# Grouped-query attention on one core: the first transposes, copies and products of the first chunk in quarters

## The chip, the cores and the metric

The kernel runs on one core of a Trainium2 chip. The metric is the device time of one execution in microseconds (us), the slowest core's (here the only one's). PE is the matrix engine, PEld its loads of weights, DVE the vector engine, ACT the scalar engine, SP the engine that issues nearly all DMAs (loads from and stores to memory). A load "lands" when the last of its data is in.

## The reference

Two independent problems, A and B, of the same shape, whose outputs are joined:

```python
B, Sq, D = 16, 32, 1024          # 512 tokens
Hq, Hkv, Sk, Dh = 32, 4, 512, 128
q = (x @ wq)                     # 512 x 1024 by 1024 x 4096
scores = einsum("bhqd,bhkd->bhqk", q, k) * Dh ** -0.5    # k, v: one head for 8 query heads
o = einsum("bhqk,bhkd->bhqd", softmax(scores), v)
out = o @ wo                     # 512 x 4096 by 4096 x 1024
```

All tensors are bfloat16. The change touches only the first microseconds of the first step, `x @ wq` of problem A.

## The kernel before

The kernel keeps PE busy with one long stream of matmuls. At the start there is nothing to multiply: the kernel loads x, transposes it on PE (its products contract over the partitions, so it puts D there), copies it from PSUM, the buffers that it has PE write to, to SBUF, where the loads land and PE's operands lie, and loads the weights. Until then PE multiplies constants ("warm-ups"; those that fill a wait between other matmuls are called "fillers").

x is loaded in chunks of two D-blocks, the first chunk in two token halves; weights follow in the order of use. All these loads are issued by SP, one after the other:

```python
load_x(0, 0, TT // 2)            # D-blocks 0 and 1, tokens 0..255
load_w0(0, 1, 0, NF // 2)        # "first weights":  D-block 0, heads 0..2
load_x(0, TT // 2, TT)           # D-blocks 0 and 1, tokens 256..511
load_w0(0, 1, NF // 2, NF)       # "second weights": D-block 0, heads 3..5
load_w0(1, 2, 0, NF)             # "third weights":  D-block 1, heads 0..5
load_x(2, 0, TT)
# ... (more weights, the rest of x by transposing DMAs; cut)
load_wq(0, 2, 0, 2)
load_k(0)                        # four transposing DMAs
load_wq(0, 2, 2, 4)
# ... (cut)
```

P is 128, TT is 4 (tokens in blocks of 128), NF is 6 (heads in the first group), HALF is 4. The start itself:

```python
def transpose_x(d0, t0, t1):
    for d, copy in ((d0, nc.vector.tensor_copy), (d0 + 1, nc.scalar.copy)):
        ps = psum.tile([P, NTOK], BF16, name="xT_ps", tag="ob")
        for tt in range(t0, t1):
            nc.tensor.transpose(ps[:, tt * P:(tt + 1) * P], x_sb[:, tt, d * P:(d + 1) * P], ident[:])
        ts = slice(t0 * P, t1 * P)
        copy(out=xT[0][:, d, ts], in_=ps[:, ts])

# first_heads(heads, dcs, t0, t1): q[h] += w[dc, h].T @ xT[dc, tokens t0..t1], one matmul per head and dc

warm_up(22)
transpose_x(0, 0, TT // 2)
warm_up(3)
first_heads((0, 1), (0,), 0, TT // 2)
transpose_x(0, TT // 2, TT)
first_heads((2,), (0,), 0, TT // 2)
warm_up(1)
first_heads((0, 1, 2), (0,), TT // 2, TT)
first_heads((3, 4, 5), (0,), 0, TT // 2)
first_heads((3, 4, 5), (0,), TT // 2, TT)
first_heads(range(0, NF - 2), (1,))       # the first that needs the third weights
# ... (cut)
```

## Time and profile before

| | before |
|---|---|
| time, median of 3 runs | 343.97 us (343.52 to 344.53) |
| span of the profiled run | 342.1 us |
| PE busy | 338.1 us, 99% of the span |
| first matmul; last matmul starts | 0.93 us; 338.74 us |
| array rate doubles, by the distances of matmuls | about 6.44 us |

The page of the kernel before: the first lines (busy time, share of the span, instructions of each engine) and the chain of work that ended last.

```profile
span 342.1 us, 5510 instructions
## 1 busy us (share of the span) xinstructions
PE 338.1 (99%) x2128; PEld 214.6 (63%) x2128; DVE 265.6 (78%) x336; ACT 185.7 (54%) x209; POOL 46.6 (14%) x206
...
## 4 chain that ended last, share of the span: by engine, by line
PE 99%; ACT 0%; issue 0%; ACTq 0%
```

PE makes up 99% of that chain. A busy PE need not be a fast PE, though: in this trace PE counts as 99% busy although the first 5.5 us of it, from 0.93 to about 6.44 us, run at half rate. The starts of matmuls tell more. The timeline of PE from 3.25 to 6.95 us (start, us from first start to last end, what, how many):

```profile
3.03 0.42 PE L515 MATMUL q_ps<-const-bfloat16-1.0 128*128 128x128 bf16 x2
3.29 0.61 PE L523 MATMUL xT_ps<-ident,x_sb 128*128 128x128 bf16 x4
3.69 0.53 PE L515 MATMUL q_ps<-const-bfloat16-1.0 128*128 128x128 bf16 x3
4.07 0.59 PE L533 MATMUL q_ps<-xT,w_sb 128*128 128x256 bf16 x2
4.44 0.63 PE L523 MATMUL xT_ps<-ident,x_sb 128*128 128x128 bf16 x4
4.87 0.42 PE L533 MATMUL q_ps<-xT,w_sb 128*128 128x256 bf16 x1
5.08 0.31 PE L515 MATMUL q_ps<-const-bfloat16-1.0 128*128 128x128 bf16 x1
5.25 1.93 PE L533 MATMUL q_ps<-xT,w_sb 128*128 128x256 bf16 x10
```

L515 is a warm-up, L523 a transpose, L533 a product. The DVE timeline shows the two copies that the products of the first and second token half wait for:

```profile
3.72 0.29 DVE L527 COPY xT<-xT_ps 128x256 bf16<-128x256 bf16 x1 [2.76 <-PE xT_ps L523]
4.90 0.29 DVE L527 COPY xT<-xT_ps 128x256 bf16<-128x256 bf16 x1 [0.89 <-PE xT_ps L523]
```

The first copy ends at 4.01 us and the product starts at 4.07; the second ends at 5.19 and the product starts at 5.25.

### The profile page before, as it was taken

To read this page: it belongs to the slowest core of one execution; us is meant where nothing else is said; L and a number is where in the kernel's file an instruction comes from. 1 tells how busy PE (TensorE), PEld (TensorE's weight loads), DVE (VectorE), ACT (ScalarE), POOL (GpSimd) and SP (SyncE) were. 2 spreads that over 40 slices of the span, in tenths; PEclk is the share of its full clock that TensorE was granted. 3 is DMA by queue.
4 is the path that set the end of the run, shared out by engine and by line. 5 is a ranking of instruction groups with operands and counts; after the bars stand their busy time and mean duration, and the time that the engine had idled before them with its cause. 6 is when DMAs were issued, how large, how long until landed. Compare 5 with 4: busy or idle time off the path is not lost.

```text
span 342.1 us, 5510 instructions
## 1 busy us (share of the span) xinstructions
PE 338.1 (99%) x2128; PEld 214.6 (63%) x2128; DVE 265.6 (78%) x336; ACT 185.7 (54%) x209; POOL 46.6 (14%) x206
## 2 busy tenths in 40 slices
PE   8999999999999999999999999999999999999996
PEld 7456666666666666666666666666666666666555
DVE  1047988888888889888888888798888888889540
ACT  2067666676666666676655554555454555555110
POOL 0001111101111111111101212222122100111100
DMA  6999999899999998999999856999439996430001
GB/s 194 253 243 183 284 261 256 173 232 269 299 234 248 238 252 231 251 304 303 281 319 259 191 125 180 283 323 211 129 104 306 350 194 139 103 96 17 17 17 33
DMA packets 128093, 71.70 MB, mean 210 GB/s; under 512 B 75840, under 2 KB 127296, under 8 KB 128064
## 3 DMA queue, kind: packets, MB, share of 16 engines
q1 hardware_dynamic: 127536, 70.21, 84.7%
q0 software_dynamic: 384, 1.05, 0.9%
q8 instruction: 17, 0.28, 0.3%
q14 instruction: 12, 0.10, 0.1%
q10 hardware_dynamic: 144, 0.07, 0.1%
HBM read 50.86 MB, written 2.10 MB: 155 GB/s over the span
## 4 chain that ended last, share of the span: by engine, by line
PE 99%; ACT 0%; issue 0%; ACTq 0%
PE f_ps L320 32%; PE q_ps L301 28%; PE ob L425 16%; PE s_ps L357 16%; PE q_ps L533 4%; PE q_ps L515 1%; PE xT_ps L523 0%; ACT o_sb L329 0%; ACTq L329 0%
## 5 line engine op out<-in xcount | busy, mean ns | idle before, releaser
L365 ACT ACTIVATE p_sb<-s_ps,shift 128x1024 bf16<-128x1024 f32 x128 | 142.6, 1114 | 97.8 <-PE s_ps L357 82.0
L376 DVE TRANSPOSE_TENSOR_REDUCE parts<-p_sb 128x32 f32<-128x1024 bf16 x128 | 158.8, 1240 | 19.2 <-ACT p_sb L365 17.6
L320 PE MATMUL f_ps<-wo_sb,oT 128*128 128x512 bf16 (+1 forms) x544 | 131.8, 366 | 0.0
L301 PE MATMUL q_ps<-xT,wq_sb 128*128 128x512 bf16 x448 | 117.4, 379 | 0.0
L425 PE MATMUL ob<-p_sb,v_sb 128*128 128x256 bf16 x512 | 76.8, 273 | 0.0
L357 PE MATMUL s_ps<-qT,kT 128*128 128x256 bf16 x512 | 76.8, 273 | 0.0
L320 PEld LDWEIGHTS <-oT 128*128 128x128 bf16 x544 | 53.2, 98 | 35.8
L357 PEld LDWEIGHTS <-kT 128*128 128x128 bf16 x512 | 56.9, 113 | 28.3
L301 PEld LDWEIGHTS <-wq_sb 128*128 128x128 bf16 x448 | 43.8, 98 | 31.7 <-DMA wq_sb<-in_A_wq_dram 0.2
L425 PEld LDWEIGHTS <-v_sb 128*128 128x128 bf16 x512 | 50.1, 98 | 20.0
L447 DVE TENSOR_TENSOR oT<-r,ob 128x512 bf16<-128x512 f32 x64 | 43.9, 686 | 21.9 <-PE ob L425 20.8
L411 DVE STREAM_TRANSPOSE r<-rall 128x512 f32<-128x512 f32 x64 | 44.2, 691 | 1.1
L309 ACT CAST qT<-q_ps 128x512 bf16<-128x512 f32 x56 | 32.6, 583 | 15.4 <-PE q_ps L301 15.4
L394 POOL COPY half<-cs 64x32 f32<-64x32 f32 x32 | 6.5, 204 | 227.4 <-DVE cs L384 227.3
L329 ACT CAST o_sb<-f_ps 128x512 bf16<-128x512 f32 (+1 forms) x17 | 9.5, 558 | 24.6 <-PE f_ps L320 24.6
L533 PE MATMUL q_ps<-xT,w_sb 128*128 128x512 bf16 (+1 forms) x70 | 15.4, 377 | 0.0
L384 DVE TENSOR_REDUCE cs<-parts 128x32 f32<-128x128 f32 x32 | 12.0, 376 | 1.1
L406 DVE RECIPROCAL rall<-sums 128x32 f32<-128x32 f32 x32 | 10.2, 320 | 3.3 <-POOL sums L403 3.3
L533 PEld LDWEIGHTS <-w_sb 128*128 128x128 bf16 x70 | 7.2, 104 | 6.9
L561 DVE CAST qT<-q_ps 128x512 bf16<-128x512 f32 x4 | 2.5, 683 | 10.2 <-PE q_ps L533 10.2
L331 POOL DMA_DIRECT2D out_dram<-o_sb x8 | 4.6, 574 | 34.7 <-ACT o_sb L329 34.6
L395 POOL TENSOR_TENSOR half<-half,cs 64x32 f32<-64x32 f32 x32 | 7.8, 242 | 2.6
(25 smaller groups left out, 46.3 us busy)
## 6 DMA issues: line engine op xcount, KB each, us to landing
v_sb<-in_A_v_cache_dram SPq DMA_DIRECT2D x16, 512.0 KB, 6.5
wq_sb<-in_B_wq_dram SPq DMA_DIRECT2D x8, 1024.0 KB, 6.0
wo_sb<-in_A_wo_dram SPq DMA_DIRECT2D x8, 1024.0 KB, 6.4
v_sb<-in_B_v_cache_dram SPq DMA_DIRECT2D x16, 512.0 KB, 4.4
wo_sb<-in_B_wo_dram SPq DMA_DIRECT2D x8, 1024.0 KB, 8.4
wq_sb<-in_A_wq_dram SPq DMA_DIRECT2D x5, 1024.0 KB, 6.3
wq_sb<-in_A_wq_dram SPq DMA_DIRECT2D x2, 512.0 KB, 5.8
kT<-in_A_k_cache_dram SPq DMA_TRANSPOSE x64, 4.5
```

Source lines behind the costliest of these rows:

```text
L301: nc.tensor.matmul(ps[:], lhsT=w[:, dc, (h % 4) * DH:(h % 4 + 1) * DH], rhs=xT[pr][:, dc, :], start=(dc == 0), stop=(dc == DC - 1),)
L309: nc.scalar.copy(out=qT[pr, g][:, :, hl, :], in_=ps[:].rearrange("p (b s) -> p b s", s=SQ),)
L320: nc.tensor.matmul(ps[:, 0:width], lhsT=oT[pr, tt][:, h, :], rhs=wo_tiles[pr, nh, h // REP][:, h % REP, off:off + width], start=(h == 0), ...
L357: nc.tensor.matmul(s_ps[:, c, :], lhsT=kT[:, i % GRP, c, :], rhs=qT[pr, g][:, b, :, :].rearrange("p h s -> p (h s)"), start=True, stop=True,)
L365: nc.scalar.activation(out=p_sb[:], in_=s_ps[:], func=ACTF.Exp, bias=shift[:], scale=SCALE)
L376: nc.vector.tensor_reduce(out=parts[k][:, q, :, :].rearrange("p c h -> p (c h)"), in_=st[i]["p"][:].rearrange("p c (h s) -> p (c h) s", s=SQ),
L384: nc.vector.tensor_reduce(out=cs[:], in_=parts.pop(k)[:].rearrange("p q c h -> p q h c"), axis=AX.X, op=ALU.add,)
L406: nc.vector.reciprocal(out=rall[:, k, :], in_=quad.pop(k)[:])
L411: nc.vector.transpose(out=r[:].rearrange("p n s -> p (n s)"), in_=rall[:, k, o * 2 * REP:(o + 1) * 2 * REP] .unsqueeze(2).to_broadcast([P, ...
L425: nc.tensor.matmul(ob[j][:, q, :], lhsT=v_sb[:, i % GRP, c, :], rhs=st[i]["p"][:, c, :], start=(c == 0), stop=(c == KC - 1),)
L447: nc.vector.tensor_tensor(out=out, in0=rcp.pop(j)[:].rearrange("p (q h) s -> p q h s", h=REP), in1=ob.pop(j)[:].rearrange("p q (h s) -> p ...
L533: nc.tensor.matmul(first_q[h][:, ts], lhsT=w0[dc // HC][:, dc % HC, h * DH:(h + 1) * DH], rhs=xT[0][:, dc, ts], start=(dc == 0 and t0 == 0 ...
```

## The change

The intent: get the first product going earlier, with fewer fillers. D-block 0 of the first token half is transposed and copied in two quarters of 128 tokens, so that the first copy is shorter and begins after one transpose rather than two; the products of heads 0 to 2 run by quarters too; and the second half's transposes stand between the two quarters. One filler goes. D-block 1 of the first half gets a PSUM buffer of its own (`spare`).

```diff
+            spare = psum.tile([P, NTOK], BF16, name="xT_ps", tag="proj")
             first_q += [psum.tile([P, NW], FP32, name="q_ps", tag="proj")[:] for _ in range(2)]
...
-            def transpose_x(d0, t0, t1):
-                for d, copy in ((d0, nc.vector.tensor_copy), (d0 + 1, nc.scalar.copy)):
+            def transpose_x(d, t0, t1, copy, ps=None):
+                if ps is None:
                     ps = psum.tile([P, NTOK], BF16, name="xT_ps", tag="ob")
... (the body unindented, warm-ups written to first_q[HALF]; cut)
             warm_up(22)
-            transpose_x(0, 0, TT // 2)
-            warm_up(3)
-            first_heads((0, 1), (0,), 0, TT // 2)
-            transpose_x(0, TT // 2, TT)
-            first_heads((2,), (0,), 0, TT // 2)
+            for tt in range(2):
+                transpose_x(0, tt, tt + 1, nc.vector.tensor_copy)
+            transpose_x(1, 0, 2, nc.scalar.copy, spare)
+            warm_up(2)
+            first_heads((0, 1, 2), (0,), 0, 1)
+            transpose_x(0, 2, TT, nc.vector.tensor_copy)
+            transpose_x(1, 2, TT, nc.scalar.copy)
+            first_heads((0, 1, 2), (0,), 1, 2)
             warm_up(1)
-            first_heads((0, 1, 2), (0,), TT // 2, TT)
-            first_heads((3, 4, 5), (0,), 0, TT // 2)
-            first_heads((3, 4, 5), (0,), TT // 2, TT)
+            first_heads((0, 1, 2), (0,), 2, TT)
+            first_heads((3, 4, 5), (0,), 0, 2)
+            first_heads((3, 4, 5), (0,), 2, TT)
```

More of the change, by code (lines that the diff above doesn't have):

```diff
@@ L515, in warm_up @@
                     nc.tensor.matmul(
-                        first_q[NF - 1][:, 0:P], lhsT=warm, rhs=warm, start=True, stop=True
+                        first_q[HALF][:, 0:P], lhsT=warm, rhs=warm, start=True, stop=True
                     )
-            def transpose_x(d0, t0, t1):
-                for d, copy in ((d0, nc.vector.tensor_copy), (d0 + 1, nc.scalar.copy)):
+            def transpose_x(d, t0, t1, copy, ps=None):
+                if ps is None:
                     ps = psum.tile([P, NTOK], BF16, name="xT_ps", tag="ob")
-                    for tt in range(t0, t1):
-                        nc.tensor.transpose(
-                            ps[:, tt * P:(tt + 1) * P], x_sb[:, tt, d * P:(d + 1) * P], ident[:]
-                        )
-                    ts = slice(t0 * P, t1 * P)
-                    copy(out=xT[0][:, d, ts], in_=ps[:, ts])
+                for tt in range(t0, t1):
+                    nc.tensor.transpose(
+                        ps[:, tt * P:(tt + 1) * P], x_sb[:, tt, d * P:(d + 1) * P], ident[:]
+                    )
+                ts = slice(t0 * P, t1 * P)
+                copy(out=xT[0][:, d, ts], in_=ps[:, ts])
             def first_heads(heads, dcs, t0=0, t1=TT):
@@ L541, in fast_path @@
             warm_up(22)
-            transpose_x(0, 0, TT // 2)
-            warm_up(3)
-            first_heads((0, 1), (0,), 0, TT // 2)
-            transpose_x(0, TT // 2, TT)
-            first_heads((2,), (0,), 0, TT // 2)
+            for tt in range(2):
[6 more added lines that the diff above has]
+            first_heads((0, 1, 2), (0,), 1, 2)
             warm_up(1)
-            first_heads((0, 1, 2), (0,), TT // 2, TT)
-            first_heads((3, 4, 5), (0,), 0, TT // 2)
-            first_heads((3, 4, 5), (0,), TT // 2, TT)
+            first_heads((0, 1, 2), (0,), 2, TT)
+            first_heads((3, 4, 5), (0,), 0, 2)
+            first_heads((3, 4, 5), (0,), 2, TT)
             first_heads(range(0, NF - 2), (1,))
-            transpose_x(2, 0, TT)
+            transpose_x(2, 0, TT, nc.vector.tensor_copy)
+            transpose_x(3, 0, TT, nc.scalar.copy)
             first_heads(range(NF - 2, NF), (1,))
```

## The prediction

> **What bounds the kernel now.** TensorE. The page gives PE 338.1 us busy of a 342.1 us span (99%), and the chain that ended last is 99% PE. Because matmul ends are modelled, I also took the starts of all 2128 matmuls from the trace and subtracted, from each start-to-start distance, the distance a matmul of that width shows when the array is fast (columns/2.4 ns plus 2.4 ns, which the trace shows throughout: 512 columns 215.7 ns, 128 columns 56 ns). After 10 us the excess is below 0.01 us per 10 us up to the last matmul: no wait on a DMA, a copy or a buffer remains there. All excess, 2.69 us, lies before 10 us. So time saved or lost at the start arrives undiminished at the end.
>
> **What the first 10 us show (timeline).** The 22 warm-ups start at 0.93 us, 107 ns apart. First x half landed 3.24; four transposes 3.29 to 3.69; three warm-ups; DVE copy (128x256, 0.29 us) ends 4.01; first multiplication 4.07; second x half landed 4.16; its transposes start 4.44; second DVE copy ends 5.19, next multiplication 5.25. 256-column matmuls are 213 ns apart until about 6.35 us and 110 ns after it: the array runs at half rate until then. The two waits for copies look like 56 ns each, but the matmul after each comes only 165 ns later instead of 213, so they cost about 10 ns each. The warm-ups already fill them.
>
> **What the change does.** PE work: one warm-up less (25 where 26 were; 107 ns slow, 56 ns fast); three 256-column matmuls become six of 128 (three more, about 2.4 ns each when fast). Transposes are unchanged. DVE's first copy becomes two of 128x128; from the measured 0.29 us (256 columns) and 0.42 us (512) I estimate 0.22 us each, on an idle engine. ACT's copies keep their size. The spare PSUM buffer swaps the two single-bank q buffers; their later users come in the same order.
>
> New timeline, estimated: transposes 3.29 to 3.69, two warm-ups to 3.90, first copy ends about 3.84 so the first quarter starts at 3.90 with no wait; three quarters to 4.22, by when the second x half is in by some 0.03 us (landing 4.16 plus 0.04 us to the load of weights); transposes to 4.65; second quarters to 4.97; warm-up to 5.08; DVE copy ends 4.97; multiplication of the second half at about 5.08 instead of 5.25. The catch-up of 165 ns disappears, so the true gain is about 0.12 us at the slow rate.
>
> If the rate doubles at the same moment as before, that progress is worth only half later: about 0.06 us, 0.02% of the time. All of it is on the critical path. The next loads used (second weights landed 4.99, used 5.84; third 6.21, used 6.80; x 7.06, used 7.66) have 0.5 us or more to spare, so they do not take it back.
>
> **What is larger than the change.** The moment of doubling. [...] An estimate from it: 1 us later costs 0.5 us, which is as wide as the three runs (343.52 to 344.53).
>
> **Predicted:** 343.9 us, 343.2 to 344.6. Faster by over 2%: 0.005; within 2%: 0.99; slower: 0.005.
>
> **Signs.** First quarter near 3.9; second-half transposes near 4.2; multiplication of the second half near 5.1; PE excess after 10 us still none; 2130 matmuls.
>
> **What would make it wrong.** The second x half landing late, stalling the transposes now placed earlier; a DVE copy slower than 0.3 us; [...].

## More of the kernel before

The starts inside a group (from the trace) are 107 ns apart for 128 columns and 213 ns for 256 until about 6.44 us, and 56 and 110 ns after it: this is the "doubling" of the rate.

## The result

| | before | after |
|---|---|---|
| time, median of 6 runs | 343.94 us (343.42 to 344.53) | 343.88 us (343.28 to 345.40) |
| ratio, 95% interval | | 1.0004 (0.9984 to 1.0024) |
| span of the profiled run | 342.1 us | 343.6 us |
| rate doubles, by the distances of matmuls | about 6.44 us | about 4.36 us |
| waits of PE after 10 us, from the starts of matmuls | none | 1.49 us at 25.3, 0.28 us at 42.5 |

A ratio is the mean time of one kernel's runs over that of the other's of the same rounds, so it is not quite the ratio of the medians.

The time is the same. The two profiles, however, differ much more than the times: the profiled run of the changed kernel was its slowest, 345.40 us, and its chain no longer is PE alone.

```profile
span 343.6 us, 5515 instructions
## 1 busy us (share of the span) xinstructions
PE 337.7 (98%) x2130; PEld 213.7 (62%) x2130; DVE 265.9 (77%) x337; ACT 185.9 (54%) x209; POOL 47.1 (14%) x206
...
## 4 chain that ended last, share of the span: by engine, by line
PE 87%; SPq 9%; DMA 2%; issue 0%; ACT 0%; ACTq 0%
```

SP's queue holds 9% of the chain, that is, loads were late. The timeline of PE of the same stretch as before (L516 is now a warm-up, L524 a transpose, L534 a product):

```profile
3.03 0.42 PE L516 MATMUL q_ps<-const-bfloat16-1.0 128*128 128x128 bf16 x2
3.29 0.61 PE L524 MATMUL xT_ps<-ident,x_sb 128*128 128x128 bf16 x4
3.69 0.42 PE L516 MATMUL q_ps<-const-bfloat16-1.0 128*128 128x128 bf16 x2
3.91 0.53 PE L534 MATMUL q_ps<-xT,w_sb 128*128 128x128 bf16 x3
4.28 0.42 PE L524 MATMUL xT_ps<-ident,x_sb 128*128 128x128 bf16 x4
4.53 0.33 PE L534 MATMUL q_ps<-xT,w_sb 128*128 128x128 bf16 x3
4.70 0.22 PE L516 MATMUL q_ps<-const-bfloat16-1.0 128*128 128x128 bf16 x1
4.97 1.14 PE L534 MATMUL q_ps<-xT,w_sb 128*128 128x256 bf16 x9
6.49 0.82 PE L534 MATMUL q_ps<-xT,w_sb 128*128 128x512 bf16 x3 [0.39 <-DMA w_sb<-in_A_wq_dram]
```

The first product starts at 3.91 us instead of 4.07, as intended. The array doubled its rate 0.45 us later, 2.1 us earlier than in the profile before: the four transposes at 4.28 us, during which this happened, take 0.42 us where they took 0.63. That earliness is then spent: the product of the second half at 4.97 us comes only when the DVE copy below is done (4.91 us), and the products with the third weights wait until 6.49 us, because those weights landed at 6.45 us.

```profile
3.62 0.36 DVE L528 COPY xT<-xT_ps 128x128 bf16<-128x128 bf16 x2 [2.66 <-PE xT_ps L524]
4.62 0.29 DVE L528 COPY xT<-xT_ps 128x256 bf16<-128x256 bf16 x1 [0.65 <-PE xT_ps L524]
```

The waits of 20 to 31 us (who waited for what: us in total, times, longest us):

```profile
PEld L301 <- DMA wq_sb<-in_A_wq_dram: 1.7, 1, 1.7
PE q_ps L301 <- DMA wq_sb<-in_A_wq_dram: 1.3, 1, 1.3
```

And the traffic of the DMA queues from 13 to 21 us in 40 slices of 0.2 us, first before, then after:

```profile
GB/s 317 164 307 264 343 407 297 274 282 300 276 283 271 288 123 44 37 38 35 17 18 112 288 262 256 291 93 106 193 193 107 49 15 125 33 33 74 128 218 289
```

```profile
GB/s 339 442 236 338 254 325 320 312 294 289 294 305 269 300 258 101 3 0 0 0 10 8 10 13 20 20 18 20 20 17 18 191 291 227 287 288 85 164 215 122
```

In both, the traffic nearly stops when the first transposing loads of keys run, at 15.8 to 16 us. The longest single packet there took 1.47 us before and 3.31 us after. With the longer stop, the loads that landed from 19.4 to 30 us did so 1.7 to 2.2 us later than in the profile before, among them the weights that PE waits for at 25.3 us (landed 25.27).

So the profiles alone give two readings. Theory A: the moment of doubling and the length of the stop are chance, and the change itself saves at most some hundredths of a microsecond. Theory B: the change brings the early doubling and the longer stop, a gain and a loss that cancel. And within theory A, a second question: does the little that the change saves reach the end, as I predicted (theory 1), or is it swallowed by a load (theory 2)?

### The profile page after: what moved, and what is told of

Read it like the earlier page. It is cut to its first block, busy times and chain, and to the rows that moved or that the text cites. A ratio compares the mean times of both kernels' runs of the same rounds, so it can differ in the third digit from the quotient of the medians.

```text
span 343.6 us, 5515 instructions
## 1 busy us (share of the span) xinstructions
PE 337.7 (98%) x2130; PEld 213.7 (62%) x2130; DVE 265.9 (77%) x337; ACT 185.9 (54%) x209; POOL 47.1 (14%) x206
## 4 chain that ended last, share of the span: by engine, by line
PE 87%; SPq 9%; DMA 2%; issue 0%; ACT 0%; ACTq 0%
PE f_ps L320 32%; PE q_ps L301 24%; PE ob L425 16%; PE s_ps L357 15%; SPq L275 6%; DMA v_sb<-in_A_v_cache_dram 2%; SPq L477 1%; SPq L471 1%; SPq L246 1%; SPq L465 0%; SPq L283 0%; ACT o_sb L329 0%; SPq L711 0%; ACTq L329 0%
## 5 line engine op out<-in xcount | busy, mean ns | idle before, releaser
L534 PE MATMUL q_ps<-xT,w_sb 128*128 128x512 bf16 (+2 forms) x73 | 14.9, 357 | 0.4 <-DMA w_sb<-in_A_wq_dram 0.4
L534 PEld LDWEIGHTS <-w_sb 128*128 128x128 bf16 x73 | 7.0, 100 | 7.3 <-DMA w_sb<-in_A_wq_dram 0.7
```

The source lines that it names most:

```text
L534: nc.tensor.matmul(first_q[h][:, ts], lhsT=w0[dc // HC][:, dc % HC, h * DH:(h + 1) * DH], rhs=xT[0][:, dc, ts], start=(dc == 0 and t0 == 0 ...
```

## The experiments

Twelve kernels ran, in three groups of four, each group on one chip. In the lists "use" is the start of the first matmul with the third weights, "landing" the landing of those weights, both from the trace. "Doubling" is the step of the granted clock as the trace records it (it recorded none in the first two profiles).

### Both kernels again: e1, g4 (before), e2, g3 (after)

No edit.

e1, kernel before: 

> The kernel before, unchanged, run again for its scatter. Theory A (what separates the two profiles is chance: the moment at which the array's rate doubles, and the length of a stop in the DMA traffic near 16 us): the time is 343.3 to 344.5 us, ratio 1.000, and the new profile shows the doubling somewhere between 4.2 and 7.7 us and a stop of 1 to 3.5 us near 16 us, either of them clearly different from the first profile's 6.35 us and 1.5 us. Theory B (the change itself causes the earlier doubling and the longer stop): doubling again within 0.3 us of 6.35 us and a stop again of about 1.5 us, no wait of PE at 25 us.

g4, kernel before: 

> The kernel before for a third profile: a doubling before 5 us here would show that the kernel before, too, then waits for the third weights at 6.1 to 6.5 us, and for its copies; one after 6 us shows again no wait for loads at all. Ratio 0.999 to 1.001: the scatter that an unchanged kernel has.

e2, changed kernel: 

> The changed kernel, unchanged, run again. Theory A: doubling and stop differ from the first profile's 4.25 us and 3.3 us, and the waits of PE (0.55 us at 6.5, 1.49 us at 25.3, 0.28 us at 42.5) shrink or vanish with them; ratio to before 0.999 to 1.001. Theory B: doubling at 4.0 to 4.5 us and the wait of 1 us or more at 25 us come back.

g3, changed kernel: 

> The changed kernel for a third profile. If the stop of 3.3 us near 16 us and the wait of 1.49 us at 25 us in its first profile were chance, as nine other profiles with stops of 1.2 to 1.8 us suggest, the stop is again 1.2 to 2 us and no wait over 0.1 us is left after 10 us. If the changed kernel brings them, they are back. Doubling anywhere from 4.2 to 7.7 us; the time fits 0.93 us + PE work + half of the slow stretch + waits either way. Ratio 0.9985 to 1.001.

Measured (the longest DMA packet of 13 to 21 us stands for the stop):

| profile | ratio to before | doubling | stop | landing | use | span | span minus use |
|---|---|---|---|---|---|---|---|
| before, first | | 6.44 | 1.47 | 6.21 | 6.80 | 342.10 | 335.31 |
| before, e1 | 0.9995 (0.9982 to 1.0007) | 6.62 | 1.82 | 6.29 | 6.87 | 342.18 | 335.31 |
| before, g4 | 1.0000 (0.9981 to 1.0018) | 4.21 | 1.81 | 6.24 | 6.29 | 341.61 | 335.32 |
| after, first | 1.0004 (0.9984 to 1.0024) | 4.36 | 3.31 | 6.45 | 6.49 | 343.61 | 337.12 |
| after, e2 | 0.9999 (0.9986 to 1.0012) | 5.67 | 1.47 | 6.19 | 6.40 | 341.70 | 335.30 |
| after, g3 | 0.9998 (0.9980 to 1.0017) | 4.53 | 1.49 | 6.27 | 6.32 | 341.64 | 335.32 |

Theory B falls. The unchanged kernel before doubles at 4.21 us in one profile and at 6.62 in another; the changed kernel at 4.36, 4.53 and 5.67. (e1 alone did not decide: its 6.62 us lies within the 0.3 us of 6.35 that theory B had named. e2 and g4 did.) The 3.31 us stop did not come back. In all fourteen profiles, whatever the kernel, the stop comes between 15.8 and 18.1 us and is 1.20 to 1.82 us, but for that one. One long stop in the ten profiles of the changed kernel and the kernels built on it, and none in the four of the kernel before and f4, cannot show whether it comes more often with the change. Runs of over 345 us do not belong to the changed kernel either: one of its 17 timed runs took 345.40 us, and one of the unchanged kernel's in the last group took 345.30 us. That run has no profile, so a long stop as its cause is not shown.

The last column says the most: from the first use of the third weights to the end, the kernel takes 335.30 to 335.32 us in every one of these profiles but the one with the long stop, where it is longer by 1.8 us, the 1.77 us of waits named above. (Among the runs below, two more exceed it: f2, 335.69 us, because it still ran at half rate from its use at 6.93 us to 7.70; and f3, 335.57 us, because PE waited 0.25 us at 41.2 us for a tile of v that landed at 41.12.) So the whole effect of the change is what it does to the moment of that first use, and this can be read in each profile. Two of them make a clean pair, both with an early doubling. PE at the end of its start, kernel before (g4), then changed kernel (g3):

```profile
4.98 1.14 PE L533 MATMUL q_ps<-xT,w_sb 128*128 128x256 bf16 x9
6.29 1.04 PE L533 MATMUL q_ps<-xT,w_sb 128*128 128x512 bf16 x4 [0.17 <-DMA w_sb<-in_A_wq_dram]
```

```profile
5.00 1.14 PE L534 MATMUL q_ps<-xT,w_sb 128*128 128x256 bf16 x9
6.32 0.82 PE L534 MATMUL q_ps<-xT,w_sb 128*128 128x512 bf16 x3 [0.17 <-DMA w_sb<-in_A_wq_dram]
```

In both, PE runs out of products with the first D-block and waits, `[0.17 <-DMA w_sb...]`, until the third weights land; the idle time shown is less than the true delay of 0.33 us, because the ends of the matmuls before it are modelled. The spans are 341.61 and 341.64 us: that is when the weights landed, 6.24 and 6.27 us, plus the same 0.05 us to the matmul. In this pair, with an early doubling, the change is worth nothing.

With a late doubling PE comes to the third weights after they have landed. Here e1 (before) and e2 (after) can be compared, and the second is early enough in its slow stretch for the products to show their turn:

```profile
4.04 0.58 PE L533 MATMUL q_ps<-xT,w_sb 128*128 128x256 bf16 x2
4.42 0.63 PE L523 MATMUL xT_ps<-ident,x_sb 128*128 128x128 bf16 x4
...
5.22 2.03 PE L533 MATMUL q_ps<-xT,w_sb 128*128 128x256 bf16 x10
```

```profile
3.88 0.53 PE L534 MATMUL q_ps<-xT,w_sb 128*128 128x128 bf16 x3
4.34 0.61 PE L524 MATMUL xT_ps<-ident,x_sb 128*128 128x128 bf16 x4
...
5.17 2.05 PE L534 MATMUL q_ps<-xT,w_sb 128*128 128x256 bf16 x12
```

The changed kernel's first product starts at 3.88 us instead of 4.04. But the second half's transposes, whose turn would have been at 4.20 us (three quarters 107 ns apart after 3.88), start at 4.34, because the second half of x landed at 4.29 us. At the third of the second-half products, once the distances have settled, the two traces give 5.598 us (e1) and 5.593 us (e2): nothing is left of the warm-up saved. The three profiles of the changed kernel have this landing at 4.23, 4.29 and 4.10 us, and only the last was in time. As a check against the time: shifting e1's use of 6.87 us back by half the 0.95 us by which e2 doubled earlier gives 6.39 us, and e2's use is 6.40.

### One warm-up less, without quarters: f4

```diff
-            warm_up(3)
+            warm_up(2)
```
(in the kernel before)

> The kernel before with one of its three warm-ups ahead of the first multiplication taken away: the saving of PE work that the change makes, without its quarters. If a warm-up only fills the wait for the DVE copy, the first multiplication still starts at 4.04 to 4.07 us and the second at 4.21 to 4.23 us, the catch-up is gone and nothing is gained: 0.00 us. If PE work at the start counted as such, both come 0.1 us earlier. Time: ratio 0.999 to 1.001 either way; the trace decides. It is also one more sample of the moment of doubling and of the stop near 16 us for the order of loads of the kernel before.

Measured: ratio 0.9993 (0.9980 to 1.0006). The timeline of PE:

```profile
3.67 0.42 PE L515 MATMUL q_ps<-const-bfloat16-1.0 128*128 128x128 bf16 x2
4.04 0.58 PE L533 MATMUL q_ps<-xT,w_sb 128*128 128x256 bf16 x2
4.42 0.63 PE L523 MATMUL xT_ps<-ident,x_sb 128*128 128x128 bf16 x4
```

The first product starts at 4.042 us and the second at 4.210, against 4.041 and 4.209 in e1. So a warm-up taken away alone gains nothing: it only filled the wait for the copy, and the copy sets the time. With the quarters the first product came at 3.88 us. This profile, with the order of work of the kernel before, doubled at 5.34 us, and its third weights (landed 6.23 us) were used at 6.28 us, at once on landing.

### The transposes not between the quarters: f3

```diff
             first_heads((0, 1, 2), (0,), 0, 1)
+            first_heads((0, 1, 2), (0,), 1, 2)
             transpose_x(0, 2, TT, nc.vector.tensor_copy)
             transpose_x(1, 2, TT, nc.scalar.copy)
-            first_heads((0, 1, 2), (0,), 1, 2)
```
(in the changed kernel)

> The changed kernel with one part undone: the second half's transposes come after both quarters instead of between them. With a late doubling: transposes of the second half start at 4.53 us, the DVE copy of them ends at 5.27 us, the multiplication of the second half starts at 5.33 us and settles about 0.1 us later than in a profile of the changed kernel with as late a doubling (5.17 us). With an early doubling the wait for that copy grows from 0.2 us to 0.35 us. Time: within 0.15 us of the changed kernel, ratio 0.999 to 1.001, not to be resolved by the rounds.

Measured: ratio 1.0005 (0.9992 to 1.0018), doubling 6.17 us.

```profile
3.88 0.85 PE L534 MATMUL q_ps<-xT,w_sb 128*128 128x128 bf16 x6
4.52 0.63 PE L524 MATMUL xT_ps<-ident,x_sb 128*128 128x128 bf16 x4
...
5.33 1.76 PE L534 MATMUL q_ps<-xT,w_sb 128*128 128x256 bf16 x10
```

The transposes of the second half start at 4.52 us, the product of the second half at 5.33 us, and the third such product at 5.703 us. That is 0.11 us later than in e2, and also 0.11 us later than in the kernel before (e1: 5.598). So, in one profile of each, quarters without the moved transposes are a loss of 0.11 us at the slow rate. The rounds can't resolve it, as expected. This profile also has a wait after 10 us, without a long stop (its longest packet near 16 us took 1.46 us): 0.25 us at 41.2 us for a tile of v that landed at 41.12 us. In e2 the same tile landed at 38.83 us and was used at 40.61.

### Twenty more warm-ups: e4

```diff
-            warm_up(2)
+            warm_up(22)
```
(in the changed kernel)

> The changed kernel with 20 more warm-ups before the first multiplication, a known extra of 20 x 56 ns = 1.12 us at the fast rate. Theory 1 (nothing behind the start absorbs a shift, as I predicted): +1.1 us, ratio 1.0033. Theory 2 (in most runs PE catches up with the loads of the first 45 us, so a shift of the start is partly swallowed by those waits): +0.2 to +0.7 us, ratio 1.0005 to 1.002, and no wait for weights at 6.5 us.

Measured: 345.10 us (344.40 to 346.40), ratio 1.0038 (1.0023 to 1.0053), that is 0.8 to 1.8 us. A delay at the start reaches the end, as theory 1 has it, and the 0.2 to 0.7 us of theory 2 is outside the interval. The third weights were long there (landed 6.21, used 8.13 us). So loads do not set the pace of the start in general: pushing it back costs the full 1.1 us, or a little more. What is left open is only the other direction, a start pulled forward; that is the next run. (In the profiled run the last store took 2.7 us to land where it took 1.6 in the profile before, so its span holds 1.1 us that do not belong to the warm-ups.)

### A larger saving at the start: g1 and g2

```diff
             load_x(0, 0, TT // 2)
-            load_w0(0, 1, 0, NF // 2)
             load_x(0, TT // 2, TT)
+            load_w0(0, 1, 0, NF // 2)
...
             warm_up(22)
+            transpose_x(0, 0, 2, nc.vector.tensor_copy)
+            ps1 = psum.tile([P, NTOK], BF16, name="xT_ps", tag="ob")
+            transpose_x(1, 0, 2, None, ps1)
+            transpose_x(0, 2, TT, nc.vector.tensor_copy, spare)
+            transpose_x(1, 2, TT, None, ps1)
+            nc.scalar.copy(out=xT[0][:, 1, :], in_=ps1[:])
+            first_heads((0, 1, 2), (0,), 0, 2)
+            first_heads((0, 1, 2), (0,), 2, TT)
+            first_heads((3, 4, 5), (0,))
... (the changed kernel's lines from warm_up(2) to first_heads((3, 4, 5), ...) removed)
```

g1: 

> A start with a larger saving: the second half of x is loaded ahead of the first weights, all eight transposes run in a row, and the three remaining fillers and the quarters are gone (22 warm-ups in all, 3 fewer than in the changed kernel). Theory 1 (PE work alone counts): with a late doubling the first multiplication comes at 4.1 to 4.2 us, that of the second half at 4.8 us instead of 5.1, and the kernel gains 0.15 us on the changed one. Theory 2 (the landing of the third weights, 6.1 to 6.45 us in all ten profiles so far, is a floor under the start): PE reaches those weights early and waits for them, 0.1 to 0.7 us where the doubling is early and less where it is late; the matmul that uses them starts at 6.15 us or later in any case and the time stays within 0.1% of before. The first weights, now third in the queue, may land after 4.2 us and make a new wait of up to 0.3 us.

g2, the same with the order of loads of e3 below: 

> The same with the reordered key loads, the candidate for a version better than both: ratio 0.9985 to 1.0005, no wait at 22 to 30 us, whatever the moment of doubling. With intervals of 0.13% either side I expect no clear win over the kernel before.

Measured: g1 343.88 us, ratio 1.0007 (0.9987 to 1.0027); g2 343.44 us, ratio 0.9998 (0.9977 to 1.0019), and no wait after 10 us in either profile. The timeline of PE in g1:

```profile
3.24 0.99 PE L524 MATMUL xT_ps<-ident,x_sb 128*128 128x128 bf16 x8
4.17 1.48 PE L535 MATMUL q_ps<-xT,w_sb 128*128 128x256 bf16 x9
6.31 0.82 PE L535 MATMUL q_ps<-xT,w_sb 128*128 128x512 bf16 x3 [0.65 <-DMA w_sb<-in_A_wq_dram]
```

All three fillers and the quarters are gone, and the products start at 4.17 us (doubling 4.03 us in this profile). Then PE has nothing more to multiply and waits until 6.31 us for the third weights, which landed at 6.26; from the starts of matmuls the delay is 0.82 us (0.45 us in g2, landing 6.15). The spans are 341.63 and 341.51 us against g4's 341.61 us of the unchanged kernel; g2's 0.10 us less is the 0.10 us by which its third weights landed earlier, and from that landing to the end all three take 335.36 to 335.37 us. Theory 2 holds in this direction: a start pulled forward ends at the landing of the third weights. g2, the candidate for a version better than both, is not shown to be better.

### Loads issued earlier, from two engines: f1

```diff
             load_x(0, 0, TT // 2)
-            load_w0(0, 1, 0, NF // 2)
+            load_w0(0, 1, 0, NF // 2, nc.scalar)
             load_x(0, TT // 2, TT)
-            load_w0(0, 1, NF // 2, NF)
+            load_w0(0, 1, NF // 2, NF, nc.scalar)
+            nc.scalar.preload_act_table_set("natural_log_exp_and_others")
```
(in e3, that is with its order of key loads, which is given below; the preload moved down from the top, and `load_w0` takes the engine)

> The changed kernel with the reordered key loads of the run before, and with the first two loads of weights issued by ACT ahead of its table load, so that every load after the first is issued 0.5 to 1 us earlier. If the landing of the second half of x limits the moved transposes (in one profile of the changed kernel it landed at 4.29 us and its first transpose came at 4.34 us, 0.14 us after its turn), it lands by 3.9 us here, the transposes start on their turn at 4.20 us, and the multiplication of the second half settles 0.1 us earlier; the third weights land by 5.8 us instead of 6.1 to 6.45 us and no wait for them is left. Gain 0.1 us in a profile with a late doubling, 0.3 to 0.6 us with an early one; ratio 0.998 to 1.000. If the traffic and not its issue is the limit, the third weights still land at 6.1 us or later and nothing moves.

Measured: 344.25 us (343.71 to 345.63), ratio 1.0022 (1.0007 to 1.0038): slower by 0.2%, clear of the noise. The first half of x, issued at 0.86 us as always, landed at 3.76 us instead of 3.04 to 3.25, so that PE stood idle before the first transposes, which start at 3.80 us; the first weights, issued 0.04 us before it, landed ahead of it, at 3.35. The second half of x landed at 4.47 us and not by 3.9, as I had expected. And the third weights, issued at 1.86 us instead of 2.84, landed at 6.38 us, no earlier. I had not expected the first two; the last is what the expectation gives for "the traffic and not its issue": 0.98 us earlier in issue, and nothing in landing. The load that everything waits for came 0.5 us or more later. Whether the second engine did it or only the order, with weights now ahead of x, was not separated. The profiled run was the fastest of the six (343.71 us) and used the third weights at 6.53 us, so that the 0.5 us more of the median run is not seen in it.

### No first warm-ups: f2

```diff
-            warm_up(22)
```
(in the changed kernel)

> The changed kernel without its 22 first warm-ups, which end just as x lands. They are no work that the result needs, so if only work counted, the time would be the same or lower. [...] +0.5 to +1.8 us, ratio 1.002 to 1.005. This tells how much more the moment of doubling weighs than the 0.06 us of the change.

Measured: 344.51 us (343.96 to 344.71), ratio 1.0017 (1.0004 to 1.0030), or about +0.6 us. The first matmul starts at 3.14 us, when x is there, and the rate doubles at 7.70 us. The 22 products of constants, useful to nobody, are worth about ten times the 0.06 us that I gave the change: in the one profile without them the doubling came at 7.70 us, later than in any profile that has them (4.03 to 6.70 us). The cost is at the low end of the +0.5 to +1.8 us that I expected, which were only my estimate.

### The loads around 25 us: e3

```diff
-            load_k(0)
+            load_k(0, slice(0, GRP // 2))
             load_wq(0, 2, 2, 4)
+            load_k(0, slice(GRP // 2, GRP))
```
(in the changed kernel)

> The changed kernel with the load of two more heads' weights put ahead of the last two of the first four key transposes, so that it is issued about 2.5 us earlier. If the wait at 25 us is one for that load alone, the load lands 2 to 3 us earlier against the matmul that needs it, no wait of over 0.1 us is left at 22 to 30 us, and runs that had it gain up to 1.5 us: ratio 0.998 to 1.000, highest run below 344.6 us. If instead the whole stream of loads is too slow, the wait moves to the key tiles (matmuls of the scores at 25 to 29 us) and the time stays.

Measured: 343.44 us (343.30 to 343.98), ratio 0.9994 (0.9981 to 1.0007), doubling 4.56 us, stop 1.53 us. The weights that the first profile of the changed kernel waited for landed at 20.7 us and were used at 23.5: 2.8 us to spare, where e2 had 1.1 us (22.6 and 23.7). The key tiles moved behind them kept 3.5 us (21.3 and 24.8). This would have covered a stop 1.9 us longer, but the long stop did not occur, so that it would have saved that run is argued, not shown; and the time is not shown to be better.

## Why the prediction was right

The time (343.88 us against 343.9 predicted) and "within 2%" were right, because the change is too small to show; a forecast of no effect would have been as right. That the two agree to 0.02 us is luck: the gain of 0.06 us that the forecast contained is found in no pair of profiles that doubled at a like moment. Point by point:

- *PE bounds the kernel, and after 10 us nothing else waits.* Shown in e1, g4, e2 and g3: 335.30 to 335.32 us from the first use of the third weights to the end. Wrong in the first profile of the changed kernel, which waited 1.77 us after 10 us; what stands out there is a DMA stop of 3.31 us that no other profile has. Wrong in f3's profile too (0.25 us at 41.2 us).
- *The change saves about one warm-up.* One warm-up fewer ran (2130 matmuls, as foretold), but at a like moment of doubling the second half's products came no more than 0.01 us earlier for it: the third of them starts at 5.593 us in e2 against 5.598 in e1, the first at 4.97 (first profile) and 5.00 us (g3) against 4.98 in g4. f4 (a filler less, without the quarters) and f3 (the quarters without the moved transposes) gain nothing either.
- *The first quarter near 3.9 us without a wait.* 3.91, 3.88 and 3.88 us. The two short copies took 0.225 and 0.215 us against 0.22 estimated.
- *The second half's transposes near 4.2 us, x in by some 0.03 us.* Half right: 4.28, 4.34 and 4.20 us. A margin of 0.03 us was read from one landing; the landings of the changed kernel's profiles spread over 0.19 us. In e2 this wait took back all of the saving. It was on my list of what could go wrong.
- *"The next loads used ... have 0.5 us or more to spare, so they do not take it back."* This is the step that failed. The slack was read from a profile with a late doubling and is no property of the loads. When the rate doubles early, PE reaches the third weights before they land: g4, g3, f4 and e3 use them 0.05 us after landing. Then "All of it is on the critical path" is false, and the 0.06 us is 0.
- *The moment of doubling is larger than the change.* Shown: 4.03 us (g1) to 6.70 us (e4) among the profiles that begin with the 22 warm-ups; what sets it among these was not shown. I had put its worth at half the shift; below about 5.4 us the landing cuts that off too (6.28 us, a typical landing plus 0.05, lies 0.59 us before e1's use, which an array doubling 1.2 us before e1's 6.62 would reach).
- *Not in the prediction:* that a copy, not a filler, would limit the second half after an early doubling. In g4 and g3 the copy ended at 4.92 and 4.95 us and its product came at 4.98 and 5.00 us.

What the change is worth, then: nothing with an early doubling; with a late one, by an estimate that no profile shows, up to 0.05 us if x lands in time (half of the 107 ns of a warm-up), and nothing in the one such profile that I have. Neither could be resolved in the times: an unchanged kernel measured against itself gives 0.9995 and 1.0000 with intervals of 0.12% and more on either side, which is 0.4 us. What stays open is what makes the DMA traffic stop when the first key transposes run, and why once for 3.31 us.

## What to carry to other kernels

Slack that is read off one profile belongs to that run's timing (in the kernel before, the third weights landed 0.59 us before their use in the first profile and 0.05 us in g4): before building on it, ask what the waits look like if the engine in front were a microsecond faster, and look for a run in which it was. Where an engine is saturated to the end, find the point from which the rest takes a constant time in every profile without a later wait; the effect of a change at the start is its effect on that point, and it can be read to 0.02 us where the times scatter by 1 us. Taking a filler away gained nothing while what it filled got no shorter (f4: 4.042 us against 4.041 in e1), and here the next load was the floor under it (g1: landed 6.26 us, used 6.31).

## What else the traces showed

- The moment of doubling limits what can be measured: between e1 (6.62 us) and g4 (4.21 us), the same kernel, it is worth 0.57 us of span, nearly ten times the 0.06 us forecast here; half of the shift would be 1.2 us, but the landing of the third weights (6.24 us in g4, used at 6.29) cuts off the rest. Against the whole it is small: all that the starts of PE's matmuls lose against the distances of the fast rate is 2.7 us of 342 in the first profile.
- The traffic of all loads nearly stops while the first key transposes are under way: 1.2 to 1.82 us in thirteen profiles here, 3.31 us in one (the longest packet), starting between 15.8 and 18.1 us. A second such stop comes in all fourteen, at 39.4 to 42.0 us, with a longest packet of 1.45 to 1.76 us. The cause was not tested, nor that the transposes are it.
- In f1 the most urgent load landed at 3.76 us instead of 3.04 to 3.25 when a second engine had issued another 0.04 us before it (one profile; the order of the loads was changed with it).
- In the trace of the kernel before, a matmul that waited 56 ns for a copy is followed by the next after 165 ns instead of 213, so that such a short wait cost only some 10 ns of array time at the half rate. At the full rate it is not so: after the wait for the third weights in g3 the next start comes after 226 ns instead of 216. In sums over starts one must look at the matmul after next.
